# Two thirds of the first expert's input product as 2x2 blocks with seven products, in one fused attention and two-expert kernel

## The chip, the core and the metric

One core of one Trainium2 chip runs the whole program. The metric is device time in microseconds. Five engines work beside one another, each through a queue of its own: TensorE (PE, with its weight loads PEld), VectorE (DVE), ScalarE (ACT), GpSimd (POOL) and SyncE (SP), which issues the transfers.

## The reference

Attention with a causal mask over 2 batches, 12 heads, 448 positions and 64 features; its output, as 896 tokens of 768 features, goes through a first expert and then a second.

```python
scores = scale * np.matmul(q, k.transpose(0, 1, 3, 2))      # (2, 12, 448, 448)
scores = np.where(mask, -1000000000.0, scores)
attn = np.exp(scores - np.max(scores, axis=-1, keepdims=True))
attn = attn / (np.sum(attn, axis=-1, keepdims=True) + 1e-09)
x = np.matmul(attn, v)            # transposed and reshaped to (896, 768)
...
h = x @ w_in                      # 768 -> 2048
x = (h - np.tanh(h)) @ w_out      # 2048 -> 768
...
x = (x @ w_a) * (x @ w_b) @ w_o   # 768 -> 1536 -> 768
```

## The kernel before

**Arithmetic.** Each operand of a product is held as two parts of a shorter float, high and low, and each product of two tiles is three matmuls: high by high, high by low, low by high (`matmuls`, L246 to L255; the matmul itself is L251). All tensors of the experts are held with features on partitions, tokens on columns: 896 columns, which are two batches of 448 or pieces of 512 and 384 (`BATCHES`, `PIECES`).

**Weights.** A weight tile is a block of 768 x 128 numbers (`block`). It passes through a pipeline that `advance` (L231) pushes on by one step of each: two DMAs on SP into one of three raw buffers (`load_part`, L145), a cast `top` on ACT (`magnitude`, L154), an operation on the bits on DVE (`bits`, L168), the high part on ACT (`split_high`, `wh`, L215) and the low part (`split_low`, `wl`, L224), on POOL during attention and on DVE behind it. There are five weight slots (`WB`) and four tiles `t` (`TP`). `plan` says in which order the tiles are split.

**Attention.** Twelve steps of a pair of heads each. What each engine does, and in which order, is written out by hand in the text `ORDER` (L23): scores (S01, S2, S3: PE, L342), masking with the row's minimum (L: DVE, L354), exponentials with row sums (X: ACT, L363, and an instruction that reads out the sum), transposes of the exponentials into PSUM (T: PE, L377), copies of them to SBUF (C, `keep_p`: ACT at L385 for the pairs of row block and head in `ACT_KEEPS`, DVE at L387 for the others), the product with v (V: PE, L403), the chain of the reciprocals of the row sums (A on POOL, I on DVE, W on POOL, R on PE, K on ACT at L430, result `y`), the division (D: DVE, L435) and the split of the result x into high and low (H: ACT, L441; J: POOL or DVE). Among these stand steps of the first expert: `f` issues two matmuls of its input product on batch 0 (`fill`), `g` a following step of its gate, `w`, `m`, `b`, `h` and `l` the steps of the weights' pipeline.

**Experts.** Behind attention a scheduler orders the instructions of all engines. Expert 1 goes in groups of feature chunks of 128, `GROUPS1` = 5, 6, 5. A chunk is 18 matmuls for each piece of columns, then the gate h - tanh(h) and its split into high and low (`hidden`, L509 to L515). Then the group's part of the output product: six tiles of `w_out`, three matmuls for each chunk of the group and piece, added up in `part` (L617, L619). The five chunks of the first group have done their batch 0 in attention. `y_terms` makes from expert 1's result, split into 2x2 blocks (feature halves by batches), the seven right-hand operands for expert 2.

Expert 2 takes two chunks of `w_a` or of `w_b` as a unit of 2x2 blocks and makes the product by seven turns (`turn`, L676) in place of eight; a turn is nine matmuls of 448 columns. `combine` (L183) forms the weights' sums and differences on DVE, `turn` adds the results up in PSUM and on DVE. Twelve units, then the product with `w_o`.

## Time and profile before

| | us |
|---|---|
| median of three runs | 579.69 (578.95 to 579.82) |
| the profiled execution | 582.26 |
| its span | 580.6 |
| PE busy | 571.5 (98%) |
| DVE busy | 347.6 (60%) |
| ACT busy | 306.2 (53%) |
| POOL busy | 72.8 (13%) |
| granted TensorE clock, mean | 0.997 |

Times are microseconds from the span's start, if not said otherwise. In a timeline the columns are the start, the duration, the engine, line and operation, what it writes and reads, the shape, and in brackets how long the engine stood idle just before and what ended that. A duration holds a part that lies under the next instruction of the same engine, so that the step from one start to the next start is shorter than the duration where an engine doesn't wait. In a table of windows each row is a stretch: its bounds and length, then for PE, PEld, DVE, ACT and POOL the busy time and the instructions (x), then the granted clock, the DMA share and GB/s. The chain of waits is followed back from the last instruction, or from the end of a window, to what released it.

### The profile page before, as it was taken

The page shows a single profiled execution, that of the slowest core. Times are in us where ns is not written, and L with a number is a line of the kernel's source. Part 1 is how long each engine was busy: PE and PEld are TensorE (multiplying, and loading weights), DVE is VectorE, ACT ScalarE, POOL GpSimd, SP SyncE. Part 2 cuts the span into 40 slices and gives each one's busy share as a digit, 9 for nine tenths or more (in the row PEclk, how much of TensorE's full clock was granted, in tenths as well). Part 3 has the DMA queues.
Part 4 walks back from the last instruction along what each step waited for, and adds up shares of the span by engine and source line. Part 5 has one row for each costly group of instructions (what it writes and reads, how often), then busy time and mean ns, then how long its engine had stood idle before and what let it go on. Part 6 is the DMA issues. An engine that isn't in the chain of part 4 may idle for free.

```text
span 580.6 us, 8654 instructions
## 1 busy us (share of the span) xinstructions
PE 571.5 (98%) x3206; PEld 498.7 (86%) x3206; DVE 347.6 (60%) x702; ACT 306.2 (53%) x625; POOL 72.8 (13%) x91
## 2 busy tenths in 40 slices
PE   8999999899999999999999999999999999999997
PEld 4777787789988888888899999999999998899996
DVE  5787786418425554444559896868787688931000
ACT  4999897518555552224544474555654548631100
POOL 4788675100000000000000000000000000000000
PEclk9999999989999999999999999999999999999999
DMA  7544532416543332223331034334343535410000
GB/s 228 167 113 140 169 86 83 142 49 215 176 152 109 109 109 91 90 92 110 108 109 54 29 106 139 109 108 130 122 130 109 163 115 188 132 65 33 32 33 32
DMA packets 70826, 64.94 MB, mean 112 GB/s; under 512 B 13952, under 2 KB 70016, under 8 KB 70784
## 3 DMA queue, kind: packets, MB, share of 16 engines
q1 hardware_dynamic: 70784, 64.40, 35.1%
q8 instruction: 25, 0.41, 0.3%
q14 instruction: 17, 0.14, 0.1%
HBM read 61.63 MB, written 2.75 MB: 111 GB/s over the span
## 4 chain that ended last, share of the span: by engine, by line
PE 90%; ACT 5%; DVE 1%; DMA 1%; issue 1%; POOL 0%; SPq 0%; ACTq 0%; DVEq 0%
PE s L251 42%; PE t L251 18%; PE h L251 13%; PE o L251 9%; ACT p L363 3%; PE o L403 3%; PE t L377 2%; PE s L342 2%; DMA qk<-in_q 1%; DVE t L168 1%; ACT pt L385 1%; DMA raw<-in_moe_w_out 1%; DVE p L354 0%; PE t L422 0%; ACT top L154 0%
## 5 line engine op out<-in xcount | busy, mean ns | idle before, releaser
L215 ACT CAST wh<-t 128x384 fp32r<-128x384 f32 (+2 forms) x118 | 70.9, 626 | 92.5 <-PE t L251 38.0
L224 DVE TENSOR_TENSOR wl<-t,wh 128x384 fp32r<-128x384 f32 (+2 forms) x113 | 75.5, 686 | 68.7 <-ACT wh L215 67.9
L154 ACT CAST top<-raw 128x768 f16<-128x768 bf16 (+1 forms) x70 | 73.5, 1050 | 59.4 <-DVE t L168 31.5
L251 PE MATMUL s<-xl,wh 128*128 128x512 f32 (+1 forms) x183 | 69.6, 381 | 0.0
L251 PE MATMUL s<-xh,wh 128*128 128x512 f32 (+1 forms) x183 | 69.5, 380 | 0.0
L251 PE MATMUL s<-xh,wl 128*128 128x512 f32 (+1 forms) x183 | 69.5, 381 | 0.0
L168 DVE SCALAR_TENSOR_TENSOR t<-raw,top 128x768 int32<-128x768 int32 (+1 forms) x70 | 68.1, 977 | 1.2 <-ACT top L154 0.5
L251 PE MATMUL s<-gwh,wh 128*128 128x448 f32 (+1 forms) x165 | 62.3, 378 | 0.0
L251 PE MATMUL s<-gwl,wh 128*128 128x448 f32 (+1 forms) x165 | 62.3, 378 | 0.0
L251 PE MATMUL s<-gwh,wl 128*128 128x448 f32 (+1 forms) x165 | 62.3, 378 | 0.0
L363 ACT ACTIVATE p<-p,m 112x448 f32<-112x448 f32 (+3 forms) x96 | 49.7, 525 | 7.5 <-DVE m L354 7.5
L354 DVE CUSTOM_DVE_ANT_0 p<-s,mask 112x448 f32<-112x448 f32 (+3 forms) x96 | 37.7, 442 | 8.6 <-POOL qkl L324 4.1
L251 PEld LDWEIGHTS s<-xh,wl 128*128 128x128 f32 x183 | 34.4, 188 | 5.3
L251 PEld LDWEIGHTS s<-xl,wh 128*128 128x128 f32 x183 | 34.3, 188 | 5.2
L251 PEld LDWEIGHTS s<-xh,wh 128*128 128x128 f32 x183 | 34.3, 188 | 5.1
L251 PE MATMUL t<-xh,wh 128*128 128x384 f32 (+1 forms) x99 | 34.9, 353 | 0.0
L251 PE MATMUL t<-xh,wl 128*128 128x384 f32 (+1 forms) x99 | 34.7, 350 | 0.0
L251 PE MATMUL t<-xl,wh 128*128 128x384 f32 (+1 forms) x99 | 34.6, 350 | 0.0
L251 PEld LDWEIGHTS s<-gwh,wl 128*128 128x128 f32 x165 | 30.9, 187 | 4.3
L251 PEld LDWEIGHTS s<-gwh,wh 128*128 128x128 f32 x165 | 31.0, 188 | 4.2
L251 PEld LDWEIGHTS s<-gwl,wh 128*128 128x128 f32 x165 | 31.0, 188 | 4.1
L377 PE MATMUL t<-ident,p 112*112 112x112 f32 x202 | 29.9, 267 | 2.9 <-ACT y L430 1.8
(148 smaller groups left out, 1196.0 us busy)
## 6 DMA issues: line engine op xcount, KB each, us to landing
raw<-in_moe_w_out SPq DMA_DIRECT2D x48, 383.2 KB, 3.6
raw<-in_moe_w_in SPq DMA_DIRECT2D x32, 383.2 KB, 4.5
raw<-in_moe_w_a SPq DMA_DIRECT2D x24, 383.2 KB, 3.6
raw<-in_moe_w_b SPq DMA_DIRECT2D x24, 383.2 KB, 3.6
raw<-in_moe_w_out SPq DMA_DIRECT2D x12, 255.5 KB, 3.6
qk<-in_q SPq DMA_DIRECT2D x12, 224.0 KB, 2.7
qk<-in_k SPq DMA_DIRECT2D x12, 224.0 KB, 3.8
v<-in_v SPq DMA_DIRECT2D x24, 112.0 KB, 2.6
```

Source lines behind the costliest of these rows:

```text
L154: nc.scalar.copy(out=tops[i % len(tops)][:, 0:nk, :, 1], in_=top[:, :, :, 2])
L168: nc.vector.scalar_tensor_tensor(out=ts[i], in0=low[:, :, :, 0], scalar=13, in1=top, op0=ALU.logical_shift_right, op1=ALU.bitwise_or)
L215: nc.scalar.copy(out=halves[j][0], in_=x)
L224: engine.tensor_tensor(out=lo, in0=source(j), in1=hi.bitcast(F32), op=ALU.subtract)
L251: nc.tensor.matmul(o, a, b_, start=j == 0 and not go_on, stop=j == n - 1, skip_group_check=True)
L342: nc.tensor.matmul(sc[i, c][e], a[r, 0, cs], b_[r, 1, :n], start=x == 0, stop=x == len(terms) - 1)
L354: nc.vector.tensor_tensor_reduce(out=p[:, e], in0=s, in1=mask[:QC, S - n:], scale=-scale, scalar=3.0e38, op0=ALU.add, op1=ALU.min, accum_o ...
L363: nc.scalar.activation(out=p[:, e], in_=p[:, e], func=ACTF.Exp, bias=least[i][:, c, e:e + 1], scale=-1.0, accum_out=sums[i][:, c, e:e + 1],)
L377: nc.tensor.transpose(out=pst[:QC, x * QC:(x + 1) * QC], in_=blk, identity=ident[:QC, :QC])
L385: nc.scalar.copy(out=out_, in_=in_)
L403: nc.tensor.matmul(o[64 * e:64 * e + 64, cs], vt[:, k_, e, :], p.rearrange("s c q -> s (c q)"), start=k_ == 0, stop=k_ == 2 * h + 1, skip_ ...
```

## The change

The 16 chunks of expert 1 go in groups of 4, 6 and 6. The first group is computed as before, with four fills in attention and not five. The 12 chunks of the other two groups form six units of 2x2 blocks, and each unit is computed by the seven turns that expert 2 uses: 63 matmuls of 448 columns take the place of 36 of 512 and 36 of 384. The seven right-hand operands of x are formed on DVE from high plus low (`x_sums`) and split again on ACT and DVE (`x_terms`) while the first group runs. `turn` hands its results to `gate` in expert 1 and to `times` in expert 2. The output products of the second and third group go in pieces of 512 and 384, where the last group went in 448s before. `ACT_KEEPS` gets a fourth member, `low_x` goes to DVE for five pairs and not one, one weight tile's low part in attention goes to DVE, and the text `ORDER` is another throughout.

```diff
-v.2 w S3.0 S01.0 L3.0 L0.0 S2.0 X3.0 L1.0 q.3 L2.0 X0.0 T31.0 X1.0 T30.0 C31.0 C30.0 T00.0 X2.0 T01.0 Q0.2 q.4
...
+v.2 w S3.0 L3.0 S01.0 L0.0 S2.0 X3.0 L2.0 q.3 T31.0 X0.0 T30.0 L1.0 X2.0 C30.0 T20.0 C20.0 Q0.2 q.4 S3.1 C31.0
...
-    NFILL = 5
+    NFILL = 4
...
-    ACT_KEEPS = {(0, 0), (2, 0), (3, 0)}
+    ACT_KEEPS = {(0, 0), (2, 0), (3, 0), (3, 1)}
...
-    GROUPS1 = [5, 6, 5]
+    GROUPS1 = [4, 6, 6]
...
+    def pair(w, f):
+        units.append(len(tiles))
+        tiles.extend([block(w, slice(0, DM), f), block(w, slice(0, DM), f + 1)])
+
+    def in_turn(u0, early):
+
+        n = len(units) - u0
+        out = [(0, 1), (0, 5), (1, 1), (1, 5)] if early else [(0, 1)]
+        for u in range(n):
+            ms = [2, 5, 6, 3, 7, 4] if early and u == n - 1 else [2, 6, 5, 7, 3, 4]
+            for m in ms:
+                if m == 4 and u + 1 < n:
+                    out.append((u + 1, 2 if early and u == 0 else 1))
+                out.append((u, m))
+        seen = set()
+        stages.append([(u0 + u, m) for u, m in out if not ((u, m) in seen or seen.add((u, m)))])
+        plan.extend(stages[-1])
...
+        u0 = len(units)
+        for fc in range(f0, f0 + g, 1 if f0 == 0 else 2):
+            if f0:
+                pair(w_in, fc)
+            else:
+                whole(block(w_in, slice(0, DM), fc))
+        if f0:
+            in_turn(u0, False)
...
         j = at["halve"]
         if j >= at["high"]:
             return
-        engine = nc.gpsimd if in_attention else nc.vector
+        engine = nc.gpsimd if in_attention and j not in (5,) else nc.vector
...
             def low_x(i):
                 b, kk = pairs[i]
                 hi, lo = [t[kk][:, b * S:(b + 1) * S] for t in (xh, xl)]
-                engine = nc.vector if i in (5,) else nc.gpsimd
+                engine = nc.vector if i in (4, 7, 8, 10, 11) else nc.gpsimd
                 engine.tensor_tensor(out=lo, in0=xs.pop(i), in1=hi.bitcast(F32), op=ALU.subtract)
...
+    def x_sums(kk):
+
+        sums = []
+        for k, tag in ((kk, "gwh"), (kk + NK, "gwl")):
+            t = g_full[0].tile([128, NT], F32, tag=tag, name="xsum")
+            nc.vector.tensor_tensor(out=t, in0=xh[k].bitcast(F32), in1=xl[k].bitcast(F32), op=ALU.add)
+            sums.append(t)
+        (b11, b12), (b21, b22) = [[t[:, cs] for cs in BATCHES] for t in sums]
+        minus(b11, b12, b11)
+        minus(b12, b22, b12)
+        minus(b22, b22, b11)
+        minus(b21, b21, b22)
+        return {5: b11, 7: b12, 6: b22, 4: b21}
+
+    def x_terms():
+
+        for kk in range(NK):
+            halve(xh[kk][:, B1], xl[kk][:, B1], sums[kk][5])
+            yield
+        rights_of(xh, xl)
+        later = []
+        for kk in range(NK):
+            for m in (6, 7, 4):
+                if kk == 0 or kk == 1 and m != 4:
+                    halve(*room(kk, m), sums[kk][m])
+                    yield
+                else:
+                    later.append((kk, m))
+        while not over:
+            yield
+        for kk, m in sorted(later, key=lambda x: (6, 7, 4).index(x[1])):
+            halve(*room(kk, m), sums[kk][m])
...
+    def gate(u, q, x, on_chip):
+
+        f, b = 2 * u + q // 2, q % 2
+        if f not in made:
+            made.add(f)
+            new_g(f)
+        th = etile()
+        nc.scalar.activation(out=th, in_=x, func=ACTF.Tanh)
+        minus(x if on_chip else th, x, th)
+        halve(gh[f, b], gl[f, b], x if on_chip else th)
...
+    def times(u, q, x, on_chip):
+
+        f, b = u // 2 * 2 + q // 2, q % 2
+        if u % 2 == 0:
...
+    def turn(u, m, outcome):
+
+        wh, wl = next_weights()
+        if m in (1, 2, 5):
+            {1: X, 2: Y, 5: Z}[m][u] = next_bank()[:, :S]
+        o = {1: X, 6: X, 7: X, 4: X, 2: Y, 5: Z, 3: Z}[m][u]
+        product(o, [((wh[:, kk], wl[:, kk]), rights[kk][m]) for kk in range(NK)], go_on=m in (6, 7, 4, 3))
+        if m in (1, 6, 5):
+            c = {1: c1, 6: c2, 5: z}[m][u] = etile()
+            nc.scalar.copy(out=c, in_=o)
+        elif m == 4:
+            outcome(u, 2, o, False)
+        else:
+            c, q = {2: (c1, 0), 7: (z, 3), 3: (c2, 1)}[m]
+            add(c[u], o)
+            outcome(u, q, c.pop(u), True)
+        at["done"] += 1
+        advance()
...
+        if gi == 0:
+            sums = {}
+            for f in range(g):
+                if f < NK:
+                    sums[f] = x_sums(f)
+                if f % 2 == 0:
+                    two = [g_full[0].tile([128, NT], F32R, tag=x, name=x) for x in ("gwh", "gwl")]
+                gh[f, 1], gl[f, 1] = [t[:, BATCHES[f % 2]] for t in two]
+                for _ in hidden(held[f], B1, gh[f, 1], gl[f, 1], next_bank()[:, :S], now, now):
                     pass
-                at["done"] += 2 * (cs.stop == NT)
+                at["done"] += 2
                 advance()
-        for dm in DM_ORDER if final else range(KD):
+            terms = x_terms()
+        else:
+            u0 = stages[gi - 1][0][0]
+            for u, m in stages[gi - 1]:
+                turn(u, m, lambda u, q, x, on_chip: gate(u - u0, q, x, on_chip))
+            at["done"] += at["done"] % 2
+        made.clear()
+        for i, dm in enumerate(DM_ORDER if final else range(KD)):
             wh, wl = next_weights()
-            for b, cs in enumerate(BATCHES if final else pieces):
+            for b in (1, 0) if gi and i == 0 else (0, 1):
+                cs = PIECES[b] if gi else BATCHES[b]
                 y = next_bank()[:, :cs.stop - cs.start]
                 if gi:
-                    gs = [(gw[f][0][:, cs], gw[f][1][:, cs]) for f in range(g)]
+                    gs = [[x[:, cs] for x in gw[f]] for f in range(g)]
                 else:
                     gs = [(gh[f, b], gl[f, b]) for f in range(g)]
                 product(y, [((wh[:, f], wl[:, f]), gs[f]) for f in range(g)])
...
+                    next(terms, None)
                 else:
-                    nc.vector.tensor_tensor(out=part[dm][:, cs], in0=y, in1=part[dm][:, cs], op=ALU.add)
-                if final:
+                    add(part[dm][:, cs], y)
+                if final and i:
                     y_terms(dm, b)
```

ACT in the middle of attention, one cycle of a pair. `pt` are the copies of transposed exponentials (L385 before, L407 after), `p` the exponentials (L363, L385), `y` the transposed reciprocals (L430, L452), `wh` a weight's high part (L215, L237). Before:

```order
L385 COPY pt_103<-t 112x3x112
L385 COPY pt_102<-h 112x336
L363 ACTIVATE p,sum<-p,m 112x448 x2
L385 COPY pt_103<-h 112x4x112
L363 ACTIVATE p,sum<-p,m 112x112 x2
L363 ACTIVATE p,sum<-p,m 112x224 x2
L363 ACTIVATE p,sum<-p,m 112x336 x2
L430 COPY y<-t 128x448
L441 CAST xh<-x 128x448
L385 COPY pt_103<-t 112x3x112
L385 COPY pt_102<-h 112x336
```

After:

```order
L452 COPY y<-t 128x448
L385 ACTIVATE p,sum<-p,m 112x112 x2
L385 ACTIVATE p,sum<-p,m 112x336 x2
L385 ACTIVATE p,sum<-p,m 112x224 x2
L407 COPY pt_103<-t 112x4x112
L463 CAST xh<-x 128x448
L237 CAST wh<-t 128x768
L407 COPY pt_102<-t 112x336
L407 COPY pt_103<-t 112x3x112
L452 COPY y<-t 128x448
L407 COPY pt_103<-t 112x4x112
```

In after a cycle has two copies of 112x4x112 and a cast `wh`, in before one such copy and no cast.

DVE in the second group of expert 1, the input product. Before, `e` is h - tanh(h), `gwl` its low part, `wl` the weight's low part, `t` the weight from its bits:

```order
L513 TENSOR_TENSOR e<-s,e 128x512
L515 TENSOR_TENSOR gwl<-e,gwh 128x512
L224 TENSOR_TENSOR wl<-t,wh 128x768
L513 TENSOR_TENSOR e<-o,e 128x384
L168 SCALAR_TENSOR_TENSOR t<-raw,top_84 128x768
L515 TENSOR_TENSOR gwl<-e,gwh 128x384
L513 TENSOR_TENSOR e<-s,e 128x512
```

After, L680 adds a turn's result, L588 is a difference of the gate, L585 a low part, L246 half a weight slot's low part, L206 and L212 weight sums:

```order
L680 TENSOR_TENSOR e<-s,e 128x448
L588 TENSOR_TENSOR e<-e 128x448
L680 TENSOR_TENSOR e<-s,e 128x448
L246 TENSOR_TENSOR wl<-t,wh 128x384 x2
L585 TENSOR_TENSOR gwl<-e,gwh 128x448
L186 SCALAR_TENSOR_TENSOR t<-raw,top_84 128x768
L588 TENSOR_TENSOR e<-e 128x448
L206 TENSOR_TENSOR t<-t 128x384
L680 TENSOR_TENSOR e<-s,e 128x448
L246 TENSOR_TENSOR wl<-t,wh 128x384 x2
L588 TENSOR_TENSOR e<-s,e 128x448
L585 TENSOR_TENSOR gwl<-e,gwh 128x448
```

The pieces of 512 and 384 have become 448 and half tiles of weights, and the additions and weight sums are new.

ACT near the end of attention. `top` are the weights' casts that wait for their DMAs. Before:

```order
L385 COPY pt_103<-t 112x4x112
L512 ACTIVATE e<-h 128x448
L441 CAST xh<-x 128x448
L154 CAST top_83<-raw 128x640
L385 COPY pt_102<-t 112x336
L385 COPY pt_103<-t 112x3x112
L514 CAST gh<-e 128x448
L154 CAST top_84<-raw 128x640
L430 COPY y<-t 128x448
L154 CAST top_83<-raw 128x640
L441 CAST xh<-x 128x448
```

After:

```order
L172 CAST top_83<-raw 128x512
L385 ACTIVATE p,sum<-p,m 112x448 x2
L172 CAST top_84<-raw 128x512
L407 COPY pt_103<-t 112x4x112
L407 COPY pt_102<-t 112x336
L385 ACTIVATE p,sum<-p,m 112x336 x2
L172 CAST top_83<-raw 128x768
L463 CAST xh<-x 128x448
L407 COPY pt_103<-t 112x3x112
L385 ACTIVATE p,sum<-p,m 112x112 x2
L407 COPY pt_103<-t 112x4x112
L452 COPY y<-t 128x448
```

In before two of the last three `top` stand directly ahead of and behind the copy `y`; in after they stand earlier, with three or more instructions between the last of them and the copy `y`.

## Rows read from the trace of the kernel before

**Rows 1.** Page, part 4: the chain of waits by line, whole span
```profile
PE s L251 42%; PE t L251 18%; PE h L251 13%; PE o L251 9%; ACT p L363 3%; PE o L403 3%; PE t L377 2%; PE s L342 2%; DMA qk<-in_q 1%; DVE t L168 1%; ACT pt L385 1%; DMA raw<-in_moe_w_out 1%; DVE p L354 0%; PE t L422 0%; ACT top L154 0%
```

**Rows 2.** Windows by stage: length, busy us per engine, granted clock, DMA share, GB/s
```profile
8.00:63.10 55.10, 53.17 (x522) 40.17 (x522) 43.28 (x170) 52.15 (x170) 42.60 (x53) 1.00 0.52 150
63.10:124.50 61.40, 58.97 (x452) 47.47 (x450) 36.62 (x100) 40.18 (x105) 25.80 (x27) 0.97 0.38 115
124.50:165.00 40.50, 40.50 (x198) 36.68 (x197) 22.78 (x31) 24.93 (x39) 1.16 (x1) 1.00 0.48 156
165.00:300.00 135.00, 135.00 (x669) 121.28 (x668) 68.00 (x96) 59.57 (x87) 0.00 (x0) 1.00 0.33 106
300.00:490.00 190.00, 190.00 (x921) 172.47 (x921) 149.98 (x267) 103.27 (x185) 0.00 (x0) 1.00 0.35 113
```

**Rows 3.** Chain pieces, three stretches (512, 384; 448; 448 columns): start, us, what
```profile
202.19 4.12 PE s L251 x18
206.31 3.14 PE t L251 x18
...
160.72 3.10 PE s L251 x15
...
335.73 1.86 PE h L251 x9
```

**Rows 4.** Chain, 20 to 63 us: by line, and one piece
```profile
by line: ACT p L363 38.2%; PE o L403 10.8%; ACT pt L385 7.3%; PE t L377 6.1%; PE s L342 5.8%; issue 5.5%; DVE t L168 4.4%; DVE p L354 3.9%; ACT y L430 3.3%; ACT xh L441 3.0%; ACT top L154 2.5%; DVE x L435 2.4%; DVE pt L387 2.2%; POOL sum L4
...
25.34 1.39 PE s L342 x18
```

**Rows 5.** ACT timeline, two stretches: start, us, instruction, [idle before <-releaser]
```profile
25.38 0.53 ACT L385 COPY pt<-t 112x448 f32<-112x448 f32 x1
25.80 0.45 ACT L385 COPY pt<-h 112x336 f32<-112x336 f32 x1
27.25 0.44 ACT L385 COPY pt<-t 112x336 f32<-112x336 f32 x1 [1.01 <-PE t L377]
...
40.05 0.84 ACT L215 CAST wh<-t 128x768 fp32r<-128x768 f32 x1
40.77 0.58 ACT L441 CAST xh<-x 128x448 fp32r<-128x448 f32 x1
```

**Rows 6.** DVE timeline at 25 us, one copy
```profile
24.98 0.62 DVE L387 COPY pt<-t 112x448 f32<-112x448 f32 x1 [1.48 <-PE o L403]
```

**Rows 7.** PE timeline: the first matmul of expert 1
```profile
63.08 0.45 PE L251 MATMUL h<-xh,wh 128*128 128x448 f32 x1
```

**Rows 8.** Timeline near the end of attention, PE and ACT
```profile
113.99 0.37 PE L251 MATMUL h<-xh,wl 128*128 128x448 f32 x1
114.76 0.90 ACT L154 CAST top<-raw 128x640 f16<-128x640 bf16 x1 [1.96 <-DMA raw<-in_moe_w_out]
...
116.11 0.78 PE L377 MATMUL t<-ident,p 112*112 112x112 f32 x3 [1.76 <-ACT y L430]
```

**Rows 9.** Windows after that stop
```profile
116.00:118.00 2.00, 1.89 (x7) 1.60 (x7) 0.51 (x1) 0.98 (x2) 0.00 (x0) 0.55 1.01 340
118.00:120.00 2.00, 2.00 (x7) 0.97 (x6) 0.00 (x0) 0.00 (x0) 0.00 (x0) 0.60 0.09 30
```

**Rows 10.** DVE timeline, expert 2
```profile
440.06 0.55 DVE L224 TENSOR_TENSOR wl<-t,wh 128x384 fp32r<-128x384 f32 x1
440.52 0.62 DVE L674 TENSOR_TENSOR gl<-e 128x448 f32<-128x448 f32 x1
441.06 0.55 DVE L224 TENSOR_TENSOR wl<-t,wh 128x384 fp32r<-128x384 f32 x1
...
442.99 0.95 DVE L168 SCALAR_TENSOR_TENSOR t<-raw,top 128x768 int32<-128x768 int32 x1
443.86 0.62 DVE L674 TENSOR_TENSOR g<-e 128x448 f32<-128x448 f32 x1
```

**Rows 11.** Window of the densest DVE
```profile
440.00:460.00 20.00, 20.00 (x99) 18.16 (x98) 18.55 (x35) 11.93 (x23) 0.00 (x0) 1.00 0.37 119
```

More of the change, by code (lines that the diff above doesn't have):

```diff
@@ L97, in block, with whole @@
         return w[r, c * W:(c + 1) * W].rearrange("(k p) n -> p k n", p=128)[:, :, 1:]
+    plan, units, stages = [], [], []
+    def whole(block_):
+        plan.append((len(tiles), None))
+        tiles.append(block_)
+    def pair(w, f):
[13 more added lines that the diff above has]
+        plan.extend(stages[-1])
@@ L122, in attention_moe_moe2 @@
-    plan += turns
+            pair(w, f)
+    in_turn(u0, True)
     for dm in range(KD):
         for h in range(2):
-            plan.append((len(tiles), None))
-            tiles.append(block(w_o, slice(h * DM, (h + 1) * DM), dm))
+            whole(block(w_o, slice(h * DM, (h + 1) * DM), dm))
     last_use = {}
     for j, (i, m) in enumerate(plan):
-        for x in (i,) if m is None else (base + 2 * i, base + 2 * i + 1):
+        for x in (i,) if m is None else (units[i], units[i] + 1):
@@ L201, in split_high @@
         full = m is None
-        if (i if full else base + 2 * i + int(m not in (1, 2))) >= at["bits"]:
+        if not full and j > at["halve"]:
             return
-        if full or at["slots"] % 2 == 0:
+        if (i if full else units[i] + int(m not in (1, 2))) >= at["bits"]:
+            return
+        if full:
+            at["slots"] += at["slots"] % 2
+        if at["slots"] % 2 == 0:
             if at["slots"] // 2 >= at["done"] // 2 + WB:
@@ L709, in attention_moe_moe2, with split_g @@
-    for u, m in turns:
-        if (u, m) == (NU - 1, 2):
-            split_g(0)
-        turn(u, m)
-    for f in range(1, NF2):
+            if final and i == 0:
+                y_terms(dm, 0)
+                y_terms(dm, 1)
+            at["done"] += 2
+            advance()
+            advance()
+        if gi == 0:
+            over.append(True)
+            for _ in terms:
+                pass
+    gs = {}
+    def split_g(f):
+        if f < NK:
+            t = [partp.tile([128, NT], F32R, tag="part", name="gpart") for _ in range(2)]
+        elif f < NK + KD:
+            t = [xp.tile([128, NT], F32R, tag=x, name=x) for x in ("xh", "xl")]
+        elif f < NK + KD + 2:
+            t = [xtra.tile([128, NT], F32R, tag=x, name=x) for x in ("th", "tl")]
+        else:
+            t = [g_full[0].tile([128, NT], F32R, tag=x, name=x) for x in ("gwh", "gwl")]
+        gs[f] = t
+        for cs in PIECES:
+            halve(*[x[:, cs] for x in t], g32[f][:, cs])
@@ L714, in attention_moe_moe2 @@
+    u0 = stages[-1][0][0]
+    for u, m in stages[-1]:
+        if u - u0 == NF2 - 1 and m in (2, 5, 6):
+            split_g({2: 0, 5: 1, 6: 2}[m])
+        turn(u, m, lambda u, q, x, on_chip: times(u - u0, q, x, on_chip))
+    for f in range(NK, NF2):
         split_g(f)
```

248 lines of the change are left out of this document (94 added, 154 removed).

## The prediction

> **What bounds the kernel now.** I read the chain of waits first: four groups of one line, L251, which issues every product of the two experts, hold 82% of it [rows 1]. Then the busy time by stretch [rows 2]. There are two kinds of stretch. From 124.5 us to 490 us PE is busy for every microsecond at full granted clock, so each column of matmul taken away there shortens the run by its own time, as long as DVE and ACT keep up: DVE is at 50% from 165 to 300 us (expert 1) and at 79% from 300 to 490 us (mostly expert 2, which works by seven products already). From 8 to 63.1 us, before the first matmul of expert 1 [rows 7], it is ACT that is full: 52.15 of 55.10 us, 2.95 idle, and the chain of that stretch lies on ACT's exponentials, 38% [rows 4]. Work that is added to PE there is hidden, work that is added to ACT is not. From 63.1 to 124.5 us the two mix, and PE loses time at one place only, which is below.
>
> **A, the products of expert 1.** Paces from the chain [rows 3]: 18 matmuls of 512 columns 4.12 us, 18 of 384 3.14, 15 of 448 3.10, 9 of 448 1.86 (0.207 each).
> Input product before: five chunks of group 0 in two batches, 5 x 36 x 0.207 = 37.2 us, and 11 chunks at 4.12 + 3.14 = 7.26, 79.9; 117.1 in all. After: four chunks of group 0, 29.8, and six pairs x seven turns x 1.86 = 78.1; 107.9. So **-9.2 us**. Output product before: the 5-chunk groups 6 x 2 x 3.10 = 37.2 each, the 6-chunk group 6 x 7.26 = 43.6; 118.0. After: 29.8 for four chunks and 2 x 43.6; 116.9. **-1.1 us**. Together -10.3, all on the path, since PE bounds these stretches. A pair saves only 14.52 - 13.02 = 1.50 us, because the old pieces of 512 cost less for each column than pieces of 448 do: 0.450 against 0.461 ns. That is why 12 chunks at 7/8 of the columns bring 9.0 us and no more.
>
> **B, the new order ahead of the first fill.** Up to the first matmul of expert 1 the order of before and of after hold the same exponentials. But on ACT after has nine more copies of transposed blocks (eight of 112x448: the set of copies that ACT makes has a fourth entry; the other is one of 112x336 that comes earlier), and two more casts of `wh`, since three tiles are split before the first fill and not one. One such copy takes 25.38 to 25.80 = 0.42 us of ACT's row, one cast 40.05 to 40.77 = 0.72 [rows 5]. 9 x 0.42 + 2 x 0.72 = 5.2. ACT is the full engine there, so I charge it whole: **+5.2 us**. The low end is 5.2 - 2.95 = +2.2, if the added work fills ACT's idle time [rows 2]; the high end +9, if eight pairs pay half of such a wait of ACT for a transpose as the 1.01 us in [rows 5]. The value is nearer to the low end's mechanism than to the high one's, but ACT's 2.95 us are spread over many short waits that an added copy does not fill by itself; so I take the plain sum.
> The copies leave DVE, where one lasts 0.62 us against 0.53 on ACT [rows 5, 6]. [...]
>
> **C, more of attention under that stretch.** By the first fill after has issued one block of scores S01, one S2 and a set of transposes more than before. 18 such score matmuls take 1.39 us of the chain [rows 4], the transposes some 0.3: 1.7 us of PE that is done while ACT bounds, and is missing later, where PE bounds: **-1.7 us** (bounds 0 and -1.7).
>
> **D, the stop near the end of attention.** PE ends a matmul at 113.99 + 0.37 and the next, a transpose, starts at 116.11; it waited for ACT's copy `y`, ACT stood 1.96 us for a DMA of `w_out` that the cast `top` needs, which stands right ahead of `y` in ACT's queue [rows 8]. Afterwards the granted clock is 0.55 and 0.60, half speed, the lower of the two levels, until 120 us [rows 9]; what PE does in these 4 us would take 0.45 and 0.40 of each 2 us less: (0.45 + 0.40) x 2 = 1.7. With 1.9 us stood still, 3.6 in all. In the new order the casts `top` of the `w_out` tiles stand well ahead of the last two copies `y`, with exponentials and copies in between, and none directly before; the loads are issued earlier too, and are smaller (four chunks and not five). I take it as gone: **-3.6 us**; bounds 0 (the stop comes back at another `top`) and -3.6. What is late next there is the chain of the last pair's reciprocals, which stands in both kernels.
>
> **E, DVE.** By paces [rows 10] DVE takes 0.46 us for 384 columns, 0.54 for 448, 0.87 for the bits of a tile. Group 0 is given the sums of x: six additions of 896 (1.0, twice a 448), twelve subtractions of 448 and twelve subtractions for the low halves, some 19 us. Counted along the new order, DVE's work up to the gates of group 0's first chunk is 21.2 us, and PE's up to the output product that reads them 22.1: 0.9 us to spare, two to seven for the others. In a pair stage one unit costs DVE two bits 1.74, four weight sums 1.88, seven low halves 3.29, three additions 1.62 and eight instructions of the gates 4.32: 12.85 us, against 13.02 of PE. That is 99%. Over six units any pause of DVE is a loss, but ahead of the stage DVE has 10 to 20 us of weights in hand, and the output product that follows each stage leaves it 43.6 us to catch up. The same engine ran at 18.55 of 20 us while PE was never idle [rows 11]. I charge 1.5 for group 0 and 1.0 for the two stages: **+2.5 us**; bounds 0 and +6 (a few per cent of idle DVE in 78 us, behind which PE's banks wait).
> At nothing I cost: the added copies and casts on ACT outside attention (it is at 44% from 165 to 300 us [rows 2]); the lows of x moved from POOL to DVE in attention; the larger number of loads, which stays the same in bytes; a last product in pieces of 512 and 384, which is in A. Their cover is idle ACT, DVE and DMA time under a PE that is always busy; without cover ACT's part would be the 0.4 us of a copy for each turn.
>
> **Sum.** -10.3 + 5.2 - 1.7 - 3.6 + 2.5 = **-7.9 us**. The profiled execution took 582.26 us, its span 580.6; it is 2.6 us above the median of the runs, 579.69, and the difference is taken as it is: 574.4 for a profiled one, **571.8 us** against the median.
>
> **The rivals.**
> *The first stretch isn't lengthened.* ACT's added work falls into its idle time and the stretch is limited by the exchange with PE and DVE, which the moved copies relieve. For it: DVE's copies are links of that chain too, and 2.95 us are idle. Against: 95% busy ACT. Five less: 566.6 us. Chance 0.15.
> *DVE bounds the pair stages.* If it reaches 79% as from 300 to 490 us [rows 2], a unit takes 12.85/0.79 = 16.3 us in place of 13.02, six units 19 us more than I charge: 590 us. At 93%, its share at its densest [rows 11], they take 4.8 more. The loss eats the whole 7.9 at about 87%; above that the kernel is faster, below slower. For it: gates that need ACT between two DVE instructions, twice. Against: 79% is what was asked for in that stage, not what DVE can do, since PE never waited. Slower with chance 0.10.
> *The exchange in the first stretch gets worse.* The new order strings A, I, W and R of one pair without much between, so PE and ACT wait for one another: eight pairs by 0.5 us more, +4: 575.8 us; with the stop of D back as well, 579.4. For it: ACT waits of 1.01 us in [rows 5]. Against: PE has slack there. Chance 0.24.
> *The change doesn't do what it says.* If the accumulating turns cost 0.24 us for a matmul and not 0.207, 378 of them lose 12 us and nothing is gained, about 582. Against it: expert 2's turns run at 0.207 [rows 3]. Chance 0.03.
>
> **How the numbers follow.** The forecast has 0.48. The range: the low end is the first rival, 566.5. The high end takes the worse exchange with the stop back, 579.5. Left out are most of the slower rival, the fourth and a tail below 566.5, about 0.2. A measurement of this kernel can tell some 0.2%, 1.2 us. Faster by more: forecast, first rival, nearly all of the third and a part of DVE's, 0.83. Within 0.2%: the upper end of the third, 0.06. Slower: 0.11, nearly all DVE.
>
> **What would show it.** B and C: the first matmul of L251's counterpart starts near 68.3 us and not 63.08, with ACT at 95% or more until then. D: no stretch of PE near the end of attention with the clock at 0.55 to 0.60. A: nine matmuls of a turn in 1.86 us in the chain. E: PE busy through both pair stages with DVE above 90%; idle PE, if any, in the output product of group 0, with DVE named as its releaser. The prediction is wrong if PE waits for DVE in the pair stages for more than some 6 us, or if the first fill starts before 64 or after 73 us.

## The result, and the profile after

The kernel after takes 571.27 us (median of four runs, 571.10 to 571.82) beside 579.67 for the kernel before: ratio 0.9859, 95% interval 0.9842 to 0.9876, 8.4 us faster. The forecast was 571.8. That the sum came out is not yet a reason to believe its terms, and three of the five (B, D and E) were wrong by more than 1.5 us. (The title's two thirds is a slip: 12 of the 16 chunks are three quarters.)

The page of after, busy time and the chain by line:

```profile
PE 560.6 (98%) x3152; PEld 488.1 (86%) x3152; DVE 386.7 (68%) x799; ACT 330.3 (58%) x700; POOL 65.9 (12%) x87
...
PE s L273 38%; PE t L273 20%; PE h L273 15%; PE o L273 9%; ACT p L385 4%; PE o L425 3%; PE t L399 2%; PE s L364 2%; ACT pt L407 1%; DMA raw<-in_moe_w_out 1%; DMA qk<-in_q 1%; PE t L444 1%; ACT top L172 1%; ACT y L452 0%; PE h L399 0%
```

L273 is the matmul that was L251. It still holds 82% of the chain, as in [rows 1]; PE is busy 10.9 us less, DVE 39 and ACT 24 us more. The windows of after, where those of before are [rows 2]:

```profile
8.00:66.20 58.20, 54.91 (x542) 41.23 (x543) 41.47 (x169) 56.99 (x181) 45.15 (x55) 1.00 0.54 157
66.20:119.00 52.80, 51.24 (x406) 40.23 (x405) 28.69 (x90) 37.88 (x105) 17.62 (x22) 1.00 0.34 103
119.00:160.00 41.00, 41.00 (x200) 37.15 (x199) 38.65 (x65) 27.89 (x54) 0.00 (x0) 1.00 0.30 96
160.00:240.00 80.00, 80.00 (x393) 71.93 (x392) 60.79 (x102) 44.26 (x75) 0.00 (x0) 1.00 0.43 138
240.00:323.00 83.00, 83.00 (x408) 74.70 (x407) 66.42 (x115) 48.00 (x85) 0.00 (x0) 1.00 0.30 96
```

Behind attention (119 us) PE is busy all the time, as it was before. DVE, at 56% there before in group 0 and at 50% from 165 to 300 us [rows 2], is at 94% in group 0 (119 to 160 us) and at 76 and 80% in the two others. The first matmul of expert 1, which is in [rows 7] at 63.08, and a turn of nine matmuls in the chain (start, us, what):

```profile
66.21 0.45 PE L273 MATMUL h<-xh,wh 128*128 128x448 f32 x1
...
176.53 1.86 PE h L273 x9
```

Before the experiments a second profile of the kernel before is needed, since its profiled execution was 2.6 us over its median. That is the first of them.

### The profile page after: what moved, and what is told of

The parts are those of the page before. It is cut to its first block, busy times and chain, and to the rows that moved or that the text cites. A ratio compares the mean times of both kernels' runs of the same rounds, so it can differ in the third digit from the quotient of the medians.

```text
span 570.1 us, 8702 instructions
## 1 busy us (share of the span) xinstructions
PE 560.6 (98%) x3152; PEld 488.1 (86%) x3152; DVE 386.7 (68%) x799; ACT 330.3 (58%) x700; POOL 65.9 (12%) x87
## 4 chain that ended last, share of the span: by engine, by line
PE 89%; ACT 6%; DMA 2%; issue 1%; DVE 1%; POOL 0%; SPq 0%; ACTq 0%; DVEq 0%
PE s L273 38%; PE t L273 20%; PE h L273 15%; PE o L273 9%; ACT p L385 4%; PE o L425 3%; PE t L399 2%; PE s L364 2%; ACT pt L407 1%; DMA raw<-in_moe_w_out 1%; DMA qk<-in_q 1%; PE t L444 1%; ACT top L172 1%; ACT y L452 0%; PE h L399 0%
## 5 line engine op out<-in xcount | busy, mean ns | idle before, releaser
L237 ACT CAST wh<-t 128x384 fp32r<-128x384 f32 (+2 forms) x142 | 78.8, 581 | 86.4 <-PE s L273 46.2
L246 DVE TENSOR_TENSOR wl<-t,wh 128x384 fp32r<-128x384 f32 (+2 forms) x137 | 83.1, 626 | 39.4 <-ACT wh L237 39.2
L273 PE MATMUL s<-xl,wh 128*128 128x448 f32 (+1 forms) x159 | 57.3, 360 | 0.0
L273 PE MATMUL s<-xh,wl 128*128 128x448 f32 (+1 forms) x159 | 57.0, 360 | 0.0
L273 PE MATMUL s<-xh,wh 128*128 128x448 f32 (+1 forms) x159 | 56.6, 360 | 0.0
L385 ACT ACTIVATE p<-p,m 112x448 f32<-112x448 f32 (+3 forms) x96 | 50.0, 527 | 6.1 <-DVE m L376 6.1
L273 PE MATMUL s<-gwh,wl 128*128 128x384 f32 (+2 forms) x102 | 37.1, 364 | 0.0
L273 PE MATMUL s<-gwl,wh 128*128 128x384 f32 (+2 forms) x102 | 36.9, 363 | 0.0
L273 PE MATMUL s<-gwh,wh 128*128 128x384 f32 (+2 forms) x102 | 36.4, 364 | 0.0
L273 PEld LDWEIGHTS s<-xh,wl 128*128 128x128 f32 x159 | 29.8, 188 | 2.4
L273 PEld LDWEIGHTS s<-xl,wh 128*128 128x128 f32 x159 | 29.8, 188 | 2.4
L273 PEld LDWEIGHTS s<-xh,wh 128*128 128x128 f32 x159 | 29.8, 188 | 2.3
L680 DVE TENSOR_TENSOR e<-s,e 128x448 f32<-128x448 f32 x27 | 16.7, 620 | 19.9 <-PE s L273 19.7
L273 PE MATMUL t<-xh,wh 128*128 128x448 f32 (+1 forms) x78 | 29.2, 374 | 0.0
L273 PE MATMUL t<-xl,wh 128*128 128x448 f32 (+1 forms) x78 | 29.1, 373 | 0.0
L273 PE MATMUL t<-xh,wl 128*128 128x448 f32 (+1 forms) x78 | 28.9, 373 | 0.0
L425 PE MATMUL o<-pt,v 112*64 112x224 f32 (+1 forms) x288 | 26.9, 327 | 0.0
```

What stands on the lines that cost most here:

```text
L237: nc.scalar.copy(out=halves[j][0], in_=x)
L246: engine.tensor_tensor(out=lo, in0=source(j), in1=hi.bitcast(F32), op=ALU.subtract)
L273: nc.tensor.matmul(o, a, b_, start=j == 0 and not go_on, stop=j == n - 1, skip_group_check=True)
L385: nc.scalar.activation(out=p[:, e], in_=p[:, e], func=ACTF.Exp, bias=least[i][:, c, e:e + 1], scale=-1.0, accum_out=sums[i][:, c, e:e + 1],)
L425: nc.tensor.matmul(o[64 * e:64 * e + 64, cs], vt[:, k_, e, :], p.rearrange("s c q -> s (c q)"), start=k_ == 0, stop=k_ == 2 * h + 1, skip_ ...
L680: nc.vector.tensor_tensor(out=x, in0=o, in1=x, op=ALU.add)
```

## The experiments

**1. The kernel before, profiled once more.** No edit.

> The kernel before, profiled once more. Its first profiled execution took 582.26 us, 2.6 more than its median, and holds a stop of 1.9 us near 114 us with the clock at half afterwards, which the prediction takes as gone (-3.6). Theory 1: the stop is part of every execution; it is there again, between 112 and 120 us, and the time is near 579.7 with it. Theory 2: it depends on when a transfer lands and was in that one execution; there is none or a shorter one here, the last matmul of attention is 2 to 3.6 us earlier than 124.5, and the span is near 577 to 578.5.

579.24 us, span 577.5. The stop near 114 us in its timeline, beside [rows 8], and the clock behind it, beside [rows 9]:

```profile
114.23 0.90 ACT L154 CAST top<-raw 128x640 f16<-128x640 bf16 x1 [2.00 <-DMA raw<-in_moe_w_out]
115.00 0.52 ACT L430 COPY y<-t 128x448 f32<-128x448 f32 x1
...
115.57 0.50 PE L377 MATMUL t<-ident,p 112*112 112x112 f32 x3 [1.78 <-ACT y L430]
```

```profile
116.00:118.00 2.00, 2.00 (x10) 1.30 (x10) 0.51 (x1) 0.91 (x1) 0.00 (x0) 1.00 0.86 297
118.00:120.00 2.00, 2.00 (x12) 1.85 (x11) 0.00 (x0) 0.00 (x0) 0.00 (x0) 1.00 0.05 17
```

The wait is a part of the kernel: 2.00 us of ACT and 1.78 of PE, as in the first execution. The clock at half speed is not a part of every execution: after the same stop the granted clock stays 1.00. In the first execution it is 0.50 in each half microsecond from 116.5 to 119.5 us, and 1.00 from 120 to 124. How often it comes can be read from the executions of the kernel before that were timed beside all these experiments, 38 of them. Six have a mean granted clock of 0.996 or 0.997, as the first profiled one had, and took 580.2 to 582.4 us; the other 32, at 0.999 or 1.000, took 578.3 to 580.1. None of the six was profiled, so that their low clock follows this stop is an inference. So theory 1 has the stop and theory 2 the price: of the 3.6 us in term D at most 1.8 belong to the execution that the median stands for. Where traces are compared, the text says which execution stands for before. The runs were made on several chips, on which the median of before lies between 578.92 and 579.67 us, so a distance between medians of two experiments is good to some 0.7 us; a ratio is always taken to runs of before on the same chip.

**2. The twelve chunks without the seven products.**

```diff
-        for fc in range(f0, f0 + g, 1 if f0 == 0 else 2):
-            if f0:
-                pair(w_in, fc)
...
+        for fc in range(f0, f0 + g):
+            whole(block(w_in, slice(0, DM), fc))
...
-            for u, m in stages[gi - 1]:
-                turn(u, m, lambda u, q, x, on_chip: gate(u - u0, q, x, on_chip))
+            for f in range(g):
+                w = next_weights()
+                new_g(f)
+                for cs in PIECES:
+                    for _ in hidden(w, cs, gw[f][0][:, cs], gw[f][1][:, cs], next_bank()[:, :cs.stop - cs.start], now, now):
+                        pass
```

> The kernel after with the 12 chunks of groups 2 and 3 computed without the seven products, in pieces of 512 and 384 as before, and without the sums of x; groups 4, 6, 6, the list of attention and the copies as in after. Theory (term A, E small): 12 x 7.26 = 87.1 us of PE in place of 78.1, so +9.0, less some 0.5 us that DVE costs: about 579.8 us, ratio to the kernel before 1.000. Rival (the seven products lose what they save to DVE, and the list of attention brings the gain): 572 to 574 us.

579.27 us (ten runs, 578.27 to 580.48), ratio 0.9994 (0.9981 to 1.0007): 8.0 us slower than after, and no faster than before. From the last matmul of attention to the end of expert 1 it needs 213.1 us, after 204.4: 8.7 against 9.0 forecast. PE has no idle time in that stretch:

```profile
118.50:331.60 213.10, 213.10 (x1054) 191.58 (x1052) 123.54 (x183) 103.44 (x155) 0.00 (x0) 1.00 0.35 111
```

So under the new list the gain is the seven products' own, and the regrouping and the new list together bring nothing by themselves. Whether the seven products would bring it under the old list too is what experiment 4 asks.

**3. The set of copies with three entries.**

```diff
-    ACT_KEEPS = {(0, 0), (2, 0), (3, 0), (3, 1)}
+    ACT_KEEPS = {(0, 0), (2, 0), (3, 0)}
```

> The kernel after with the twelve copies of row block 3, second head, back on DVE (the set with three entries). Theory (term B: ACT is the full engine before the first fill): eight of them lie there, 8 x 0.42 = 3.4 us; the first matmul of expert 1 comes 1.7 (half absorbed by ACT's idle time) to 3.4 us earlier than 66.2, and the time is 568 to 569.6 us. Rival (the copy belongs on ACT, and DVE is a link of the chain as well): the first matmul no earlier than 66, time 571.3 to 573 us.

570.07 us (569.34 to 572.33), ratio 0.9849 (0.9823 to 0.9875). The first matmul of expert 1 stands at 65.72, 0.5 us earlier, not 1.7 to 3.4. The window to there, to be held against the first row of after:

```profile
8.00:66.20 58.20, 53.93 (x542) 40.91 (x540) 44.18 (x172) 53.69 (x172) 45.82 (x57) 1.00 0.56 159
```

ACT works 3.3 us less and DVE 2.7 more, and the stretch is hardly shorter: ACT now stands idle where it worked. Waits up to the first matmul tell why. In a table of waits each row has the engine and what it waited for, then us in total, the number of waits and the longest:

```profile
PE t L399 <- DVE pt L409: 1.6, 2, 0.9
ACT pt L407 <- PE t L399: 1.9, 3, 1.1
```

PE waits 1.6 us for DVE's copies, for which no wait shows there in after, and ACT in turn waits 1.9 us for PE's transposes. Neither side of the expectation holds well. The theory fails on the size, the rival on the sign.

**4. The attention of before under the experts of after.**

```diff
-v.2 w S3.0 L3.0 S01.0 L0.0 S2.0 X3.0 L2.0 q.3 T31.0 X0.0 T30.0 L1.0 X2.0 C30.0 T20.0 C20.0 Q0.2 q.4 S3.1 C31.0
+v.2 w S3.0 S01.0 L3.0 L0.0 S2.0 X3.0 L1.0 q.3 L2.0 X0.0 T31.0 X1.0 T30.0 C31.0 C30.0 T00.0 X2.0 T01.0 Q0.2 q.4
...
-    ACT_KEEPS = {(0, 0), (2, 0), (3, 0), (3, 1)}
+    ACT_KEEPS = {(0, 0), (2, 0), (3, 0)}
...
-        engine = nc.gpsimd if in_attention and j not in (5,) else nc.vector
+        engine = nc.gpsimd if in_attention else nc.vector
...
-                engine = nc.vector if i in (4, 7, 8, 10, 11) else nc.gpsimd
+                engine = nc.vector if i in (5,) else nc.gpsimd
```

The list is the old one without its last nine `f` and last four `g`.

> The kernel after with the attention of before: the old list of steps without its last nine fills and last four gate steps (there are four chunks and not five), the set of copies with three entries, the low parts of x and of the weights where they were. Theory (B + C + D = -0.1 in sum): the list brings nothing, 570.5 to 572.5 us, first matmul of expert 1 near 63.1, and a stop near the end of attention. Rival (the new list is worth something of its own): 574 us or more. Other rival (it costs, and D was not in the timed runs): 568 to 569.5 us.

577.1 us (576.87 to 577.96), ratio 0.9961 (0.9946 to 0.9976), 5.8 us slower than after. The first matmul of expert 1 is early, at 62.40, as foreseen; what comes later is not. PE's timeline at the old stop, and the windows behind it:

```profile
119.00 0.43 PE L399 MATMUL t<-ident,p 112*112 112x112 f32 x1 [3.58 <-ACT y L452]
```

```profile
116.00:118.00 2.00, 0.00 (x0) 0.00 (x0) 0.00 (x0) 0.49 (x1) 0.00 (x0) 1.00 0.90 313
118.00:120.00 2.00, 1.00 (x4) 0.72 (x5) 0.16 (x1) 0.94 (x2) 0.00 (x0) 0.56 0.04 13
120.00:122.00 2.00, 2.00 (x6) 1.24 (x6) 0.35 (x1) 0.00 (x0) 0.00 (x0) 0.50 0.03 8
122.00:124.00 2.00, 2.00 (x7) 1.80 (x6) 0.00 (x0) 0.00 (x0) 0.00 (x0) 0.50 0.00 0
```

With nine fills less to run between, the stop has doubled, and the clock falls to half for six us (118 to 124 us; it is 0.73 in the next two). Behind attention PE waits for DVE, which it never does in after (its waits from 127.7 to 160 us):

```profile
PE t L273 <- DVE wl L246: 1.1, 1, 1.1
PE s L273 <- DVE gwl L541: 0.8, 1, 0.8
PE o L273 <- DVE x L457: 0.8, 1, 0.8
PE s L273 <- DVE e L539: 0.4, 1, 0.4
```

So the first rival is right here: the new attention is worth 5.8 us to this kernel, although it makes the first stretch longer. What it saves is trouble that the change would have had with the old one. Which of the list, the copies and the low parts does it, this kernel can't say, since it undoes all of them; and the nine fills were all taken from the old list's end, near the stop, so an old list shortened elsewhere might lose less, which no run tests.

With experiment 2 this makes a table of four: neither half of the change brings much without the other.

| ratio to before | plain chunks | seven products |
|---|---|---|
| old attention | 1 (before) | 0.9961 |
| new attention | 0.9994 | 0.9859 (after) |

**5. The last casts of before behind its last copy `y`.**

```diff
-C01.11 T21.11 h f C21.11 f l V1.11 V0.11 f D.11 f H.11 J.11 f f g g g g
+C01.11 T21.11 h f C21.11 f l V1.11 V0.11 f D.11 f H.11 J.11 f f g g g g m b w m b w m b w m b w
```

> The kernel before with twelve more steps at the very end of its list (m b w, four times), so that the casts of the last w_out tiles come behind the last copy y in ACT's queue and not ahead of it. Nothing else is changed. Theory (term D: the copy y waits behind a cast that waits for its DMA): PE's idle 1.8 us near 114 us is gone and no half clock follows in any execution: 577 to 578.2 us, against 579.6. Rival (PE waits there for the chain of the reciprocals in any case, or the later casts make it wait in group 0): 579 to 581 us.

578.44 us (ten runs, 577.49 to 578.84), ratio 0.9978 (0.9959 to 0.9997). The stop is gone; between 112 and 116 us PE is full:

```profile
112.00:114.00 2.00, 2.00 (x14) 1.63 (x12) 1.02 (x2) 0.51 (x1) 0.00 (x0) 1.00 0.42 147
114.00:116.00 2.00, 2.00 (x10) 1.46 (x10) 0.00 (x0) 0.00 (x0) 0.00 (x0) 1.00 0.03 8
```

The mechanism of D is shown: PE's wait of 1.8 us for `y` is gone, and all ten executions are at a mean clock of 0.999 or 1.000, where 4 of the 16 of before on this chip were not. The median is 0.5 us below before's on this chip (578.92), just above the theory's range and below the rival's. The ratio would make 1.3 us of it (1 - 0.9978 of 579), but that is about the ratio of the means (578.30 to 579.52), and the mean of before holds those four. So the wait alone is worth some 0.5 us of the 3.6 charged, and 1.3 on average with the clock. The span is 1.7 us shorter than in experiment 1, but the execution profiled here was the fastest of its ten.

**6. Eight added copies on ACT.**

```diff
+                if c == 3 and 1 <= i <= 8:
+                    nc.scalar.copy(out=warm[:QC, :S], in_=warm[:QC, :S])
```

> The kernel after with eight added copies on ACT (112 x 448, from and to a tile that nothing else uses), one behind the exponentials of each pair from 1 to 8, all but the last ahead of the first matmul of expert 1: the disputed price of ACT's time there, with nothing taken from another engine. Theory (ACT is the full engine, 1.1 us idle): 8 x 0.42 = 3.4, less what idle time takes up: first matmul of expert 1 near 69 us, time 573.6 to 574.7 us. Rival (the exchange of PE, ACT and DVE sets the pace, and ACT's load alone decides little): 571.3 to 572.5 us.

574.73 us (572.96 to 575.43), ratio 0.9914 (0.9889 to 0.9939): 3.5 us slower than after, and the first matmul of expert 1 at 68.64, 2.4 us later. The window to there:

```profile
8.00:68.60 60.60, 54.73 (x540) 40.82 (x540) 41.45 (x164) 59.20 (x188) 44.93 (x57) 1.00 0.53 152
```

ACT's busy time grew by 2.2 us with seven of the eight copies in the stretch, the stretch by 2.4. So added ACT time cost about its full length there, as the prediction had it. That a copy moved to DVE gave so little back is then DVE's price, for which experiment 3 has PE's 1.6 us of waits; no run adds such copies to DVE alone.

**7. Two added operations on DVE for each turn.** A miss, but one that tells something.

```diff
...
+        if u < NK * 2:
+            minus(scr, scr, scr)
+            minus(scr, scr, scr)
```

> The kernel after with two added subtractions of 216 columns on DVE in each of the 42 turns of expert 1 (of a tile that nothing else uses), some 0.58 us a turn, 24 us in all; a unit then asks DVE for 16.9 us against PE's 13.0. Theory (term E: work in hand ahead of a stage and the output product behind it take up what DVE falls behind): 571.5 to 577 us, PE idle a few us at the ends of the pair stages at most. Rival (DVE bounds a pair stage once it is asked for more than PE takes): six units by 3.9 us, 590 us or more.

601.42 us, ratio 1.0378 (1.0336 to 1.0420). The operations hang on nothing, and the scheduler drew them forward into the first stretch, where 82 of the 84 ran:

```profile
8.00:99.10 91.10, 69.92 (x542) 51.50 (x543) 85.34 (x251) 59.18 (x181) 45.80 (x55) 0.83 0.37 101
```

```profile
L590 DVE TENSOR_TENSOR scr<-scr 128x216 f32<-128x216 f32 x82 | 49.6, 605 | 1.3
```

The stretch is 32.9 us longer, with a mean clock of 0.83. So it says nothing on the pair stages, for which neither theory was tested. It does say that DVE's room ahead of the first fill is limited: with 44 us more busy time it ends up as the full engine, 85.34 of 91.10 us. Part of the 44 us is not the operations' own length. One of them takes 382 ns as a rule and up to 3256, and the long ones stand beside work of POOL (smallest, median and largest in the first line; then one of 3.04 us and POOL's work in that time):

```profile
L590 DVE TENSOR_TENSOR scr<-scr x84: 319/382/3256, 3.4 to 92.1; 128x216 f32<-128x216 f32 x84
27.06 3.04 DVE L590 TENSOR_TENSOR scr<-scr 128x216 f32<-128x216 f32 x1
27.63 2.23 POOL L348 TENSOR_TENSOR qkl<-qk,qkh 128x448 fp32r<-128x448 f32 x2
```

Of the 84, the 48 with no instruction of POOL beside them took 319 to 384 ns; every one above 450 ns had one beside it.

**8. Two weight splits later in the list.**

```diff
-L0.6 S2.6 R.5 K.5 b T31.6 q.10 V1.5 L2.6 X0.6 Q0.8 k.9 Q1.8 H.4 V0.5 h l L1.6 C31.6 D.5 v.8 T30.6 X1.6 S3.7
-C30.6 L3.7 S01.7 k.10 X2.6 Q2.8 T00.6 L0.7 T01.6 C01.6 A.6 I.6 C00.6 Q3.8 X3.7 T20.6 C20.6 S2.7 W.6 L1.7 q.11
-V0.6 X0.7 S3.8 J.4 X1.7 L3.8 Q0.9 R.6 K.6 T21.6 C21.6 Q1.9 T31.7 w H.5 X3.8 L2.7 T00.7 J.5 V1.6 C00.7 k.11 Q2.9
-X2.7 D.6 v.9 Q3.9 S01.8 L0.8 C31.7 S2.8 A.7 I.7 h l T01.7 C01.7 f m T20.7 C20.7 f L1.8 T30.7 f X0.8 W.7 C30.7
-T21.7 C21.7 f T31.8 X1.8 L2.8 w f Q0.10 R.7 K.7 b f S3.9 X2.8 Q1.10 L3.9 S01.9 A.8 I.8 V1.7 H.6 L0.9 J.6 h l m
+L0.6 S2.6 R.5 K.5 b T31.6 q.10 V1.5 L2.6 X0.6 Q0.8 k.9 Q1.8 H.4 V0.5 L1.6 C31.6 D.5 v.8 T30.6 X1.6 S3.7 C30.6
+L3.7 S01.7 k.10 X2.6 Q2.8 T00.6 L0.7 T01.6 C01.6 A.6 I.6 C00.6 Q3.8 X3.7 T20.6 C20.6 S2.7 W.6 L1.7 q.11 V0.6
+X0.7 S3.8 J.4 X1.7 L3.8 Q0.9 R.6 K.6 T21.6 C21.6 Q1.9 T31.7 w H.5 X3.8 L2.7 T00.7 J.5 V1.6 C00.7 k.11 Q2.9 X2.7
+D.6 v.9 Q3.9 S01.8 L0.8 C31.7 S2.8 A.7 I.7 T01.7 C01.7 f m T20.7 C20.7 f h l L1.8 T30.7 f X0.8 W.7 C30.7 T21.7
+C21.7 f T31.8 X1.8 L2.8 w f h l Q0.10 R.7 K.7 b f S3.9 X2.8 Q1.10 L3.9 S01.9 A.8 I.8 V1.7 H.6 L0.9 J.6 h l m
```

> The kernel after with two of the three splits of weight tiles (a cast wh on ACT, a low part) moved in the list from ahead of the first matmul of expert 1 to behind its second and sixth step. Theory (term B: two casts of 0.72 us lie on a full ACT): first matmul 1.4 us earlier than 66.2, and 570.0 to 571.0 us. Rival (the length of that stretch is set by the exchange and not by ACT's load): first matmul at 65.8 to 66.3, time 571 to 572 us.

572.18 us (571.63 to 574.04), ratio 0.9876 (0.9838 to 0.9914). The first matmul comes at 64.95, 1.26 us earlier, nearly the theory's 1.4; but the last matmul of attention starts at 120.19 us and not at 119.04, and the time is that of after within the noise. PE's waits in between, 65 to 120.2 us:

```profile
PE t L444 <- POOL wide L439: 1.4, 1, 1.4
PE t L399 <- DVE pt L409: 1.4, 3, 0.6
PE t L399 <- ACT pt L407: 0.2, 1, 0.2
```

The 1.3 us are given back at once behind POOL, whose queue the low parts were put into at another place, and behind DVE. A moved step does not vanish; here it cost as much where it went.

**9. Two added operations on DVE behind each gate.** They read the gate's result, so they stay in the pair stages.

```diff
...
         halve(gh[f, b], gl[f, b], x if on_chip else th)
+        y = x if on_chip else th
+        for _ in range(2):
+            minus(scr, y[:, 0:216], y[:, 216:432])
```

> The kernel after with two added subtractions of 216 columns on DVE behind each gate of expert 1, which read the gate's result and so can't move ahead of it (the operations added to each turn before could, and stood in attention). 24 gates, 48 operations of 0.29 us, 14 us in all; a unit asks DVE for 15.2 us against PE's 13.0. Theory (term E: work in hand ahead of a stage and the output product behind it take up what DVE falls behind): 571 to 575 us, PE idle up to some 3 us behind 119 us. Rival (DVE bounds a pair stage once it is asked for more than PE takes): six units by 2.2 us less what 1% of slack gives, 583 to 585 us, with PE idle 12 us or more.

569.73 us (568.72 to 571.08), ratio 0.9834 (0.9810 to 0.9858), beside 570.30 for after on the same chip: no cost. PE's waits behind 118.5 us are 0.5 us in all. The stretch of expert 1 in after, and here:

```profile
119.00:323.00 204.00, 204.00 (x997) 183.78 (x996) 165.86 (x281) 120.14 (x212) 0.00 (x0) 1.00 0.35 112
```

```profile
118.50:323.00 204.50, 204.50 (x1005) 185.23 (x1004) 178.48 (x328) 119.70 (x214) 0.00 (x0) 1.00 0.35 112
...
176.00:194.00 18.00, 18.00 (x89) 16.04 (x88) 18.00 (x35) 15.35 (x28) 0.00 (x0) 1.00 0.44 135
```

DVE takes some 12.5 us more (0.26 for each of the 48 operations, where 0.29 was estimated ahead of the run) and is full for 18 us on end (176 to 194 us), and PE does not wait. The rival, DVE as the bound, falls: 583 to 585 us forecast, 569.73 measured. The theory was too cautious as well, with 571 to 575.

**10 to 12. After once more, the set of three once more, and the set of four for every other pair.** The edit of the last:

```diff
-                if (c, e) in ACT_KEEPS:
+                if (c, e) in ACT_KEEPS and ((c, e) != (3, 1) or i % 2 == 1):
```

> The kernel after once more, beside the next two on the same chip. 571 to 572 us; the first matmul of expert 1 at 66.2 us within 0.7 (between its two executions before's moved by 0.6), and ACT waiting for a DMA of w_out near 94 us again if that wait is a part of the kernel.

> The kernel after with the set of three copies on ACT, once more, for its distance to after. Theory as the runs so far have it (the stretch is set by an exchange in which ACT's time costs nearly its full length and DVE's time too, so that moving 0.42 us of ACT to 0.54 us of DVE twelve times gives little): 0.5 to 1.5 us faster than after. Rival (ACT alone is full): 2 us or more faster.

> The kernel after with the copies of row block 3, second head, on ACT for every other pair and on DVE for the rest, to share that load between the two. Theory (both engines' time lies on the exchange, neither is full alone): between after and the set of three or a little better than both, 569.3 to 571 us. Rival (one of the two is the bound): no better than the better of the two, or as slow as the worse.

After 570.30 us (ratio 0.9843, 0.9824 to 0.9862), the set of three 570.45 (0.9842, 0.9822 to 0.9862), every other pair 568.95 (0.9826, 0.9803 to 0.9848). After's first matmul is at 66.05, and ACT waits near 94 us again, 1.26 us where it was 0.92:

```profile
95.45 0.77 ACT L172 CAST top<-raw 128x512 f16<-128x512 bf16 x1 [1.26 <-DMA raw<-in_moe_w_out]
...
96.65 0.50 PE L399 MATMUL t<-ident,p 112*112 112x112 f32 x3 [0.89 <-ACT pt L407]
```

The set of three has the shorter profiled span, 567.5 against 569.2 us, and the same median, so neither side of its expectation came true; the two spans mislead, since the execution profiled was the fastest of the four for the set of three and the slowest of the four for after. Sharing the copies out brings the lowest median of all, 1.35 us under after's and just below its forecast, but the intervals overlap, so it is a lead and not a result.

## Why the prediction was right, and where only its sum was

Spans and bounds of the two second profiles (experiments 1 and 10), from the first matmul of expert 1 and the start of the last of attention in PE's timeline (before, then after; the last of attention is the last of a group of six):

```profile
62.49 0.45 PE L251 MATMUL h<-xh,wh 128*128 128x448 f32 x1
121.97 0.73 PE L403 MATMUL o<-pt,v 112*64 112x224 f32 x6
...
66.05 0.45 PE L273 MATMUL h<-xh,wh 128*128 128x448 f32 x1
118.87 0.73 PE L425 MATMUL o<-pt,v 112*64 112x224 f32 x6
```

| us | before again | after again | difference |
|---|---|---|---|
| start to the first matmul of expert 1 | 62.49 | 66.05 | +3.56 |
| from there to the last of attention | 59.96 | 53.30 | -6.66 |
| from there to the end | 455.08 | 449.89 | -5.19 |
| span | 577.53 | 569.24 | -8.29 |

Ahead of attention's end before has issued 127 matmuls of the experts, after 102; the 25 are worth 25 x 0.207 = 5.2 us. Taken out of the second row and put into the third, these read -1.5 and -10.4.

**A, -10.3 forecast: right.** The third row gives -10.4, and with that the whole of A and nothing for E. Experiment 2 has the pairs alone at 8.0 us in the median and 8.7 in the trace, 9.0 forecast. That holds under the new attention; with the old one (experiment 4) PE waits for DVE in group 0 and stops for longer, and a part of A is lost again. Nine matmuls of a turn take 1.86 us as in [rows 3]; the rival that the turns don't run at that pace falls.

**B, +5.2 forecast, +3.6 measured** (+3.1 between the two first profiles: the first matmul of expert 1 came at 66.2 and not near 68.3). The mechanism was half of it. ACT is full there (idle for 1.10 of 58.00 us in the second row below), and added ACT time cost about its full length (2.2 us more of it, a stretch 2.4 us longer, experiment 6). The stretch in the second profiles, before and after:

```profile
8.00:62.50 54.50, 52.73 (x522) 39.92 (x520) 42.67 (x168) 51.65 (x170) 43.00 (x54) 1.00 0.53 153
8.00:66.00 58.00, 54.85 (x541) 41.07 (x542) 41.30 (x168) 56.90 (x181) 45.26 (x56) 1.00 0.56 159
```

Two steps failed. The first was to charge the work whole and leave ACT's idle time out: ACT's busy time grew by the 5.2 us of the forecast, but its idle time fell from 2.85 to 1.10. The second was to give nothing for what the copies' leaving does for DVE. Taken back (experiments 3 and 11) they shorten the stretch by 0.4 to 0.5 us where 3.4 were charged, for DVE's time there has a price too (PE's 1.6 us of waits for DVE's copies in experiment 3). With the 1.26 us of the splits in experiment 8, if the two add, that makes some 1.7 of the 3.6 us. What makes the rest no run tests: PE's busy time in the stretch grew by 2.1 us as well, by the work of term C, which the prediction took as hidden. By the time of a run neither place for these copies is shown to be the better one: the medians of after and of the set of three, on the same chip, are 570.30 and 570.45 us. The first rival, no lengthening, is wrong, and so is the range's lower end that rested on it.

**C and D, -5.3 forecast, -1.5 measured.** Here the prediction was most wrong, and the step is D's. It took the half clock of one execution, 1.7 us, for a part of every execution and subtracted it from a median that did not hold it (experiment 1); and it charged PE's wait at its full length, where taking the wait away brought 0.5 us in the median (experiment 5). And it named the wrong successor: what is late next is not the reciprocals' chain but another cast `top` that waits for `w_out`, near 94 us, ahead of two copies that PE needs. PE's waits between the two bounds, before and after:

```profile
PE t L377 <- ACT y L430: 1.8, 1, 1.8
PE t L422 <- ACT pt L385: 0.7, 1, 0.7
...
PE t L399 <- ACT pt L407: 1.3, 2, 0.9
PE t L399 <- DVE pt L409: 0.6, 1, 0.6
```

They are 2.5 us in before and 1.9 in after; the stop was made smaller and moved, by 0.6 us net. That leaves 0.9 for C, 1.7 forecast, which no run tests by itself.

**E, +2.5 forecast, 0 measured.** The reason given against the rival was right (work in hand before the stage, the output product behind it), and I then charged for the rival all the same. The count of 99% (for which weights of 384 columns were taken at 0.47 us, though the pace given is 0.46; it changes little) was made over a pair stage as if each unit's DVE work had to lie beside its own turns; in the trace it is spread over the output products too, and in the whole of expert 1 DVE has 38 us of room in 204, of which experiment 9 uses some 12.5 with no loss. The point at which DVE decides lies above that and wasn't found.

So the sum is right because D and C were too good by 3.8 us and B and E too bad by 4.1. That they cancel is luck; A alone was right in mechanism and size. What the rivals got: slower by DVE, refuted; a worse exchange, not seen, though one of the things it warned of, a stop that comes back, is there at a smaller size.

One thing the prediction did not see at all is what the new list is for. It compared the new list with the old one in the old kernel, where they are worth about the same. Under the new experts the old list, shortened at its end, costs 5.8 us more together with its copies and low parts (experiment 4): with fewer fills between attention's steps the stop doubles (3.58 us), and DVE is late in group 0 (PE's waits there are 3.1 us).

## What to carry to other kernels

Before a stall of one trace is put into a sum, look at a second execution: the wait was a part of the kernel, the clock that fell behind it did not come every time (a low mean clock shows in about one execution of six), and that was half of the term. Moving work from a full engine to a neighbour was priced at both ends here: 0.42 us of ACT ([rows 5]) against 0.54 of DVE (one such copy of before, 55.12 to 55.66 us) came out even, though added ACT time alone cost about all of its length (2.4 us for 2.2). An engine that was asked for 99% of a stage was no bound, since the stage's work could be done ahead and the next stage left it room (in experiment 9 DVE was full for 18 us on end, and PE did not wait): count over the stretch that the work may move in. And a part of a change that brings nothing alone can still be what lets the other part pay, as the table of experiment 4 shows.
